# Earlier operand loads, own weight tiles on ScalarE's queue and evenly spread conversions in a fused attention and two-MLP kernel

## The chip, the cores and the metric

One core of a Trainium2 chip runs the whole kernel. The metric is device time in microseconds (us), the median of several executions; lower is better.

## What is computed

```
scores = q @ k^T / sqrt(64) - log(448)            # 4 batches, 12 heads, 448 x 64
x      = (sigmoid(scores) @ v), heads joined       # 1792 x 768
h      = x @ w_in1;  g = h * sigmoid(h)            # 768 -> 2048
x2     = g @ w_out1                                # 2048 -> 768
h      = x2 @ w_in2                                # 768 -> 2048
g      = P(h) / (Q(h) + 1e-6)                      # P cubic in h, Q quadratic in |h|
out    = g @ w_out2                                # 1792 x 768
```

The weights arrive as the bits of 64-bit floats. Every fp32 product is made of three fp32r matmuls: each operand is split into a high part (a cast on ScalarE, ACT) and a low part (a subtraction on VectorE, DVE, or on GpSimd, POOL), and high x high, high x low and low x high are added in PSUM.

## The kernel before

Each engine works through its instructions in the order in which the program lists them; the order is written by hand, and a transfer is issued by the queue of the engine that it is written for. SP's queue (SyncE) carries nearly every transfer of this kernel. The stages, in order:

**Conversions.** `conv` (lines 141 to 163) turns one 128 x 768 piece of a weight matrix from 64-bit bits into fp32: ACT takes an absolute value (line 150), DVE does four operations (lines 151, 152, 153, 156), SP stores the result to DRAM (line 159, tensors `w0i`, `w0o`, `w1i`, `w1o`), and `conv_load` has SP fetch the piece after next (lines 133, 137). The result sits in one of the three tiles of the ring `bits`. There are 64 pieces: 16 of `w_in1`, 16 of `w_out1` (`w0o`), 32 of the second MLP. The calls are spread by hand over the first three stages.

**Attention** (loop at line 766): 24 pairs of heads `i`, each in two half steps `h`. A half step transposes q or k of a later pair (line 235, through one PSUM bank that line 238 must have drained), does two score blocks (line 245, sigmoid at line 256) and two value blocks (line 263). From pair 13 on, each half step also takes one of the 21 steps of `operands0` (lines 330 to 354), which prepares operands of the next stage: three rounds `kk` of seven operands; a round starts with three loads of attention output from DRAM (`load_b`, line 324, SP's queue) into the tiles `wf[1][0]`, `wf[1][1]` and `s34f`, the same three tiles in each round, and the first step of the round casts the first of them at once (line 283 ACT, 284 DVE). From pair 1 to 20 the first half step of a pair ends with a `conv`.

**The seven-product stage** (loop at line 821): `x @ w_in1` by a recursion with seven half-size products instead of eight, in 16 groups `g`, nine matmuls to a product. The groups 0 to 7 make tokens of batches 0 and 1, the groups 8 to 15 those of batches 2 and 3. `silu` stores the results to DRAM (`gd`, line 431, SP). Conversions stand in groups 1, 3, 5 and 9 to 15. Its end prepares the next stage: `load_wo1` (line 524, SP's queue, into a tile of `bits`) and `split_wo1` (lines 287, 288) for the first pieces of `w_out1`, `load_g` (line 510, SP's queue) and `split_gd` (lines 283, 284) for the first pieces of g.

**The second product** (`second(n)`, lines 540 to 549): 64 steps `n`, 16 to a batch, each of 18 matmuls (lines 546 to 548) from one piece of g and one piece of `w_out1`. The pieces 0 and 1 of `second` stand inside the end of the stage before; the loop at line 926 has steps 2 to 63. In step `n` it loads g for step `n + 3` and `w_out1` for step `n + 2`, splits both for step `n + 1`, and calls `conv` at line 936 whenever twice the number of conversions left is at least the number of steps left: that is in each of the steps 2 to 14, then in every other step. `w_out1` is split only in the first 16 steps; later batches use it again.

**The second MLP** (from line 950) reads the stored result back and runs 64 steps of two products. Nothing in it is changed.

Of the kernel before, what the change touches and what calls it, by code (L numbers as in the profile page):

```python
# [41 lines left out]
def attention_moe_moe(ctx: ExitStack, tc: tile.TileContext, q, k, v, w_in1, w_out1, w_in2, w_out2, a, b2, out):  # L42
    nc = tc.nc
# [278 lines left out]
    def load_b(dst, t, half, kk, second):  # L322
        b = 2 * t + second
        nc.sync.dma_start(out=dst, in_=xs[0][half * HK + kk][:, b * S : (b + 1) * S])

    def split_b(src, t, kind, kk):
        x = xop[t, kind, kk] = place[t, kind, kk]
        split(src, x)

    def operands0():  # L330
        x, y, z = wf[1][0][:, :S], wf[1][1][:, :S], s34f[:, :S]
        for kk in range(HK):
            load_b(x, 0, 0, kk, 0)
            load_b(y, 0, 0, kk, 1)
            load_b(z, 0, 1, kk, 1)
            split_b(x, 0, "11", kk)
            yield
            sub(x, y, x)
            split_b(x, 0, "T1", kk)
            yield  # L340
            sub(y, z, y)
            split_b(y, 0, "T3", kk)
            load_b(y, 0, 1, kk, 0)
            yield
            split_b(z, 0, "22", kk)
            yield
            sub(x, z, x)
            split_b(x, 0, "T2", kk)
            yield
            split_b(y, 0, "21", kk)  # L350
            yield
            sub(y, y, x)
            split_b(y, 0, "T4", kk)
            yield
# [154 lines left out]
    def load_g(n):  # L509
        if n < B * KF:  # L510
            b, c = divmod(n, KF)
            gq[n] = f448.get()
            nc.sync.dma_start(out=gq[n], in_=gd[c][b])

    def split_gd(n):
        if n < B * KF:
            t = gq.pop(n)
            gx[n] = hl.get()
            split(t, gx[n])
            f448.put(t)  # L520

    wo_in = {}

    def load_wo1(c):
        if c < KF:
            wo_in[c] = bits.get()
            nc.sync.dma_start(out=wo_in[c], in_=wd[0][c]["o"])

    def split_wo1(c):
        if c < KF:  # L530
            t = wo_in.pop(c)
            split2(t, woH[c], woL[c])
            bits.put(t)

    ring8 = (0, 1, 3, 4, 5, 7, 2, 6)

# [193 lines left out]
    with tc.manual_schedule():  # L730
# [32 lines left out]
                attn_E(i)  # L763

        first_ops = operands0()
        for i in range(NPT):
            for h in range(2):
                if h == 0:
                    mix(i + 2)
                    load_v(i + 3)  # L770
                    load_qk(i + 4)
                attn_S(i, 2 * h, attn_QK(i, 2 * h))
                p = attn_QK(i, 2 * h + 1)
                if h == 0:
                    if i == 0:
                        attn_T(1, "k")
                    attn_T(i + 1, "q")
                else:
                    hl.put(st.pop(("k", i)), st.pop(("q", i)))
                    attn_T(i + 2, "k")  # L780
                attn_S(i, 2 * h + 1, p)
                behind(*((i, 0) if h else (i - 1, 1)))
                if i >= 2 * NP + 1:
                    next(first_ops, None)
                if i == NPT - 3 and h == 0:
                    load_w1(0)
                flush()
                if i == NPT - 2 and h == 1:
                    prep_ij(0)
                    sums_12(0)  # L790
                if i == NPT - 1:
                    if h == 0:
                        prep_s12(0)
                    else:
                        prep_a22(0)
                if h == 0 and 0 < i < NPT - 3:
                    conv()
        for _ in first_ops:
            pass
# [21 lines left out]
        for g in range(NGR):  # L821
# [28 lines left out]
                operands1_late("T1")  # L850
            if fill:
                next(ops1, None)
            if g in (1, 3, 5) or g > HF:
                conv()

            p6(g)
# [17 lines left out]
                operands1_late("T3")  # L874
            if fill:
                next(ops1, None)
            if last - 3 < g < last:
                split_wo1(g - last + 2)
            if g == last:
                split_gd(0)  # L880

            if was:
# [1 line left out]
            flush()  # L884
            load_w1(g + 2)
            sums_12(g + 1)
            if last - 4 < g < last:
                load_wo1(g - last + 3)
            if g == last:
                load_wo1(3)  # L890
                split_gd(1)

            p7(g)
# [17 lines left out]
        c12(last)  # L911
        w1_s.close()
        xb_s.close()
        kt_s.close()
        wo_p, wo_s = opened("wo")
        for c in range(2, KF):
            woH.append(wo_p.tile([P, DM], F32R, tag=f"woH{c}", name=f"woH{c}"))
            woL.append(wo_p.tile([P, DM], F32R, tag=f"woL{c}", name=f"woL{c}"))
        l2_p = ctx.enter_context(tc.tile_pool(name="l2a", bufs=1, side="right", reuse_waits="tile"))
        hx.put(*fixed("hx", KD, [P, 2, BK], F32R, l2_p))  # L920
        wi_f.extend(fixed("wif", 4, [P, DM], F32, l2_p))
        split_wo1(2)
        split_gd(2)
        load_g(4)
        NL1 = B * KF
        for n in range(2, NL1):
            load_g(n + 3)
            load_wo1(n + 2)
            second(n)
            split_gd(n + 1)  # L930
            split_wo1(n + 1)
            if n % KF == KF - 1:
                results1(n // KF)
            left = NL1 - 6 - n
            if left > 0 and (len(order) - done["conv"]) * 2 >= left:
                conv()
            m = n - (NL1 - KF)
            if m == 1:
                whr.put(w0[:2], w0[2:])
# [76 lines left out]
```

## Time and profile before

| | us |
|---|---|
| median of 3 runs (1182.17 to 1184.47) | 1183.79 |
| the profiled execution | 1185.87 |
| its span, first to last instruction | 1184.1 |
| TensorE (PE) busy in the span | 1119.8 (95%) |
| DVE, ACT, POOL busy | 864.3, 633.7, 340.4 |
| mean granted TensorE clock, of full speed | 0.971 |

A stage is read here from windows: the stretch of time, the busy time of each engine in it, the clock that TensorE was granted (1.00 is 2.4 GHz, 0.50 is 1.2 GHz), and the share of the time that the 16 DMA engines were busy. Where PE's busy time is shorter than the stretch, PE waited; the waits tell for whom.

### The profile page before, as it was taken

How to read it: one execution, taken by the hardware profiler on the slowest of the kernel's cores; microseconds unless marked ns; L12 is line 12 of the kernel's file. 1: busy time of each engine (PE TensorE's matmuls, PEld its weight loads, DVE VectorE, ACT ScalarE, POOL GpSimd, SP SyncE). 2: the span in 40 equal slices, each digit the busy share in tenths (PEclk: the TensorE clock that was granted, in tenths of full speed). 3: DMA queues.
4: the chain of work that ended last, by engine and by line, in shares of the span. 5: the costliest groups of instructions: out<-in, count | busy, mean ns of one | idle time of the engine just before them, and what ended most of it. 6: DMA issues, size and time to landing. Idle time of an engine off the chain costs nothing.

```text
span 1184.1 us, 15844 instructions
## 1 busy us (share of the span) xinstructions
PE 1119.8 (95%) x5822; PEld 926.9 (78%) x5822; DVE 864.3 (73%) x1028; ACT 633.7 (54%) x1035; POOL 340.4 (29%) x246
## 2 busy tenths in 40 slices
PE   9997888999999978779999999999999999999997
PEld 5553434898889967559999898888999988889997
DVE  4665675677777826666574638888899988788996
ACT  6775666555655623232232326546666665556664
POOL 2111110000000000000000015565677666566774
PEclk9998998999989988789999999999999999999999
DMA  9998774576547747778785829000100010001001
GB/s 249 306 291 240 233 233 153 160 253 205 183 149 240 241 143 244 261 250 278 265 289 202 310 81 385 23 21 21 44 11 28 27 40 1 21 21 54 1 1 40
DMA packets 103805, 183.47 MB, mean 155 GB/s; under 512 B 8752, under 2 KB 77872, under 8 KB 103728
## 3 DMA queue, kind: packets, MB, share of 16 engines
q1 hardware_dynamic: 103024, 181.86, 47.4%
q8 instruction: 46, 0.75, 0.3%
q10 hardware_dynamic: 640, 0.59, 0.2%
q14 instruction: 31, 0.25, 0.1%
q0 software_dynamic: 64, 0.00, 0.0%
HBM read 126.06 MB, written 56.36 MB: 154 GB/s over the span
## 4 chain that ended last, share of the span: by engine, by line
PE 78%; DVE 8%; DMA 7%; ACT 4%; issue 2%; SPq 1%; POOL 0%; ACTq 0%; DVEq 0%; POOLq 0%
PE acc L677 13%; PE acc L411 10%; PE acc L680 7%; PE hb L608 6%; PE hb L606 6%; PE hb L607 6%; PE hb L263 5%; PE pair L245 4%; PE acc L547 4%; PE acc L548 4%; PE acc L546 4%; PE hb L411 3%; PE hb L235 2%; DVE bits L153 2%; DMA f<-gd 1%
## 5 line engine op out<-in xcount | busy, mean ns | idle before, releaser
L288 POOL TENSOR_TENSOR w<-wif,w 128x768 fp32r<-128x768 f32 x33 | 61.3, 1858 | 516.8 <-DVE hx L591 509.4
L256 ACT ACTIVATE f<-pair,nls 112x896 f32<-112x896 f32 x96 | 96.5, 1010 | 19.0 <-PE pair L245 19.0
L546 PE MATMUL acc<-xa,woH 128*128 128x448 f32 x252 | 95.4, 379 | 0.5 <-ACT xa L283 0.5
L547 PE MATMUL acc<-xa,woH 128*128 128x448 f32 x252 | 95.2, 378 | 0.2 <-DVE xa L284 0.2
L548 PE MATMUL acc<-xa,woL 128*128 128x448 f32 x252 | 94.6, 375 | 0.0
L263 PE MATMUL hb<-f,vs 112*64 112x448 f32 x384 | 88.2, 582 | 0.4 <-ACT f L256 0.4
L245 PEld LDWEIGHTS pair<-xa,xa 64*112 64x112 f32 x576 | 48.3, 178 | 51.3 <-issue 34.4
L283 ACT CAST xa<-f 128x448 fp32r<-128x448 f32 x64 | 35.9, 564 | 96.7 <-DMA f<-gd 96.5
L634 DVE RECIPROCAL stg<-stg 128x512 f32<-128x512 f32 (+1 forms) x28 | 84.9, 3032 | 0.0
L245 PE MATMUL pair<-xa,xa 64*112 64x448 f32 x576 | 74.6, 390 | 9.6 <-ACT f L256 9.6
L621 ACT ACTIVATE stg<-hb,absb 128x512 f32<-128x512 f32 (+1 forms) x44 | 28.0, 636 | 98.2 <-PE hb L608 98.2
L284 DVE TENSOR_TENSOR xa<-f,xa 128x448 fp32r<-128x448 f32 x64 | 40.1, 641 | 46.5 <-ACT xa L283 46.2
L411 PE MATMUL acc<-xb,wr 128*128 128x448 f32 x315 | 67.8, 366 | 0.2 <-ACT f L485 0.2
L150 ACT ACTIVATE bits<-stg 128x768 f32<-128x768 f32 x64 | 57.9, 905 | 16.4 <-DMA w1i<-bits 8.4
L288 POOL TENSOR_TENSOR wh<-wif,wh 128x768 fp32r<-128x768 f32 x31 | 57.4, 1850 | 28.2 <-DVE xio L626 25.5
L411 PEld LDWEIGHTS acc<-xb,wr 128*128 128x128 f32 x315 | 59.1, 188 | 5.8 <-issue 0.7
L153 DVE SCALAR_TENSOR_TENSOR bits<-stg,bits 128x768 int32<-128x768 int32 x64 | 61.7, 964 | 2.2
L156 DVE SCALAR_TENSOR_TENSOR bits<-stg,bits 128x768 int32<-128x768 int32 x64 | 61.6, 962 | 2.2
L677 PE MATMUL acc<-w,hx 128*128 128x512 f32 x174 | 61.4, 394 | 0.0
L677 PE MATMUL acc<-wh,hx 128*128 128x512 f32 x171 | 60.3, 393 | 0.0
L288 POOL TENSOR_TENSOR w<-wof,w 128x768 fp32r<-128x768 f32 x32 | 59.2, 1850 | 0.4 <-ACT w L287 0.2
L288 POOL TENSOR_TENSOR wh<-wof,wh 128x768 fp32r<-128x768 f32 x32 | 59.2, 1850 | 0.1
(197 smaller groups left out, 3189.6 us busy)
## 6 DMA issues: line engine op xcount, KB each, us to landing
stg<-in_moe_w_in_dram SPq DMA_DIRECT2D x32, 768.0 KB, 6.2
stg<-in_moe_w_out_dram SPq DMA_DIRECT2D x32, 768.0 KB, 5.4
gd<-f SPq DMA_DIRECT2D x64, 224.0 KB, 3.4
f<-gd SPq DMA_DIRECT2D x64, 224.0 KB, 5.8
wf<-w0i SPq DMA_DIRECT2D x32, 384.0 KB, 5.9
w0i<-bits SPq DMA_DIRECT2D x16, 384.0 KB, 4.0
w0o<-bits SPq DMA_DIRECT2D x16, 384.0 KB, 2.7
bits<-w0o SPq DMA_DIRECT2D x16, 384.0 KB, 6.2
```

What stands on the lines that cost most here:

```text
L153: nc.vector.scalar_tensor_tensor(out=ui, in0=hi, scalar=SIGN_TOP, in1=ui, op0=ALU.bitwise_and, op1=ALU.bitwise_or)
L245: nc.tensor.matmul(p[:CP, j, :S], K[rows[j], a_, c * CP : (c + 1) * CP], Q[rows[j], b_, :], start=(n == 0), stop=(n == 2),)
L256: nc.scalar.activation(t[:CP], p[:CP, :, :S], AF.Sigmoid, bias=nls[:CP], scale=QKSCALE)
L263: nc.tensor.matmul(pav[0][j * D : (j + 1) * D, :S], vs[i][:, j, c * D : (c + 1) * D], t[:CP, j], start=(c == 0), stop=(c == NCH - 1),)
L288: (eng or nc.vector).tensor_tensor(out=lo, in0=src, in1=h.bitcast(F32), op=ALU.subtract)
L411: nc.tensor.matmul(o, w_[:, w], x[:, i_, :], start=first and kk == 0 and n_ == 0, stop=kk == HK - 1 and n_ == 2, skip_group_check=not first,)
L546: nc.tensor.matmul(o, woH[c][:, w], x[:, 0, :], start=(c == 0), stop=False)
L547: nc.tensor.matmul(o, woH[c][:, w], x[:, 1, :], start=False, stop=False)
L548: nc.tensor.matmul(o, woL[c][:, w], x[:, 0, :], start=False, stop=(c == KF - 1))
L634: nc.vector.reciprocal(t0, t1)
L677: nc.tensor.matmul(acc[t][:, :BK], a_, w_[:, :BK], start=first, stop=last)
L680: nc.tensor.matmul(rest, a_, w_[:, BK:], start=first and u == 0, stop=last and u == share - 1)
```

## The change

Four edits. First, `operands0` alternates between two sets of three tiles, and the loads that open a round move out of it into `load0`, called at half steps counted back from the end of the loop: rounds 0 and 1 at the two half steps of pair 11, round 2 at the first half step of pair 17. The 21 steps of `operands0` begin one half step earlier, at the second half step of pair 12. The fourth load of a round, in its third step, stays where it was. Second, `load_g` and `load_wo1` are issued by ACT's queue instead of SP's, and `w_out1` gets four tiles of its own, `wos`, where the tiles `kept` of the stage before were; in the second product it is loaded four steps before it is split (into the tile that was just split) and g is loaded for step `n + 2`, not `n + 3`. Third, the conversions: one more in attention (pair 21), groups 0, 2, 4, 6 instead of 1, 3, 5, and in the second product a steady rate, 32 of them over the steps 3 to 58. Fourth, the tiles `hx` and `wi_f` of the second MLP are opened at step 15, when `wos` is closed.

```diff
+    sets = ((wf[1][0], wf[1][1], s34f), (wf[0][0], wf[0][1], s12f))
+
+    def load0(kk):
+        x, y, z = (t[:, :S] for t in sets[kk % 2])
+        load_b(x, 0, 0, kk, 0)
+        load_b(y, 0, 0, kk, 1)
+        load_b(z, 0, 1, kk, 1)
+
     def operands0():
-        x, y, z = wf[1][0][:, :S], wf[1][1][:, :S], s34f[:, :S]
         for kk in range(HK):
-            load_b(x, 0, 0, kk, 0)
-            load_b(y, 0, 0, kk, 1)
-            load_b(z, 0, 1, kk, 1)
+            x, y, z = (t[:, :S] for t in sets[kk % 2])
             split_b(x, 0, "11", kk)
...
-            nc.sync.dma_start(out=gq[n], in_=gd[c][b])
+            nc.scalar.dma_start(out=gq[n], in_=gd[c][b])
...
-            wo_in[c] = bits.get()
-            nc.sync.dma_start(out=wo_in[c], in_=wd[0][c]["o"])
+            wo_in[c] = wos.get()
+            nc.scalar.dma_start(out=wo_in[c], in_=wd[0][c]["o"])
...
-                if i >= 2 * NP + 1:
+                at_half = 2 * i + h - 2 * NPT
+                if at_half >= -NOPS - 2:
                     next(first_ops, None)
-                if i == NPT - 3 and h == 0:
+                for kk, when in enumerate((-NOPS - 5, -NOPS - 4, -NOPS + 6 + 1)):
+                    if at_half == when:
+                        load0(kk)
+                if at_half == -6:
                     load_w1(0)
...
-                if h == 0 and 0 < i < NPT - 3:
+                if h == 0 and 0 < i < NPT - 2:
                     conv()
...
-            if g in (1, 3, 5) or g > HF:
+            if g in (0, 2, 4, 6) or g > HF:
                 conv()
...
-            if last - 3 < g < last:
-                split_wo1(g - last + 2)
             if g == last:
+                split_wo1(0)
+                load_wo1(4)
                 split_gd(0)
...
-            if last - 4 < g < last:
-                load_wo1(g - last + 3)
+            if g == last - 1:
+                kt_s.close()
+                wos_p, wos_s = opened("wos", side="right")
+                wos.put(*fixed("wos", 4, [P, DM], F32, wos_p))
+                for c in range(4):
+                    load_wo1(c)
             if g == last:
-                load_wo1(3)
+                split_wo1(1)
+                load_wo1(5)
                 split_gd(1)
...
         split_wo1(2)
+        load_wo1(6)
         split_gd(2)
-        load_g(4)
         NL1 = B * KF
+        todo = len(order) - done["conv"]
         for n in range(2, NL1):
-            load_g(n + 3)
-            load_wo1(n + 2)
+            load_g(n + 2)
             second(n)
             split_gd(n + 1)
-            split_wo1(n + 1)
+            if n + 1 < KF:
+                split_wo1(n + 1)
+                load_wo1(n + 5)
+            if n == KF - 1:
+                wos_s.close()
+                l2_p = ctx.enter_context(tc.tile_pool(name="l2a", bufs=1, side="right", reuse_waits="tile"))
...
-            left = NL1 - 6 - n
-            if left > 0 and (len(order) - done["conv"]) * 2 >= left:
-                conv()
+            conv_to(len(order) - todo + todo * (n - 1) // (NL1 - 7))
```

## Rows read from the trace of the kernel before

**Rows 1.** Windows, whole kernel: stretch, length, busy per engine, clock, DMA share, GB/s

```profile
75.00:100.00 25.00, 25.00 (x170) 12.98 (x168) 17.35 (x26) 20.12 (x26) 4.36 (x8) 1.00 1.03 296
104.00:211.30 107.30, 85.65 (x503) 41.06 (x501) 64.52 (x98) 65.64 (x92) 10.46 (x14) 0.89 0.62 198
211.30:421.30 210.00, 205.17 (x992) 187.91 (x990) 156.25 (x259) 117.30 (x217) 0.00 (x0) 0.98 0.62 206
421.30:442.40 21.10, 14.67 (x55) 12.15 (x54) 4.26 (x8) 5.47 (x11) 0.00 (x0) 0.84 0.32 122
442.40:532.00 89.60, 68.21 (x252) 55.33 (x253) 61.27 (x83) 29.96 (x43) 0.00 (x0) 0.83 0.78 253
550.00:575.00 25.00, 25.00 (x122) 22.60 (x121) 16.58 (x25) 7.78 (x12) 0.00 (x0) 1.00 0.76 265
```

**Rows 2.** Windows, attention from pair 13: each starts with a q transpose (line 235)

```profile
101.84:116.51 14.67, 8.12 (x50) 3.96 (x49) 5.59 (x9) 5.59 (x8) 1.84 (x3) 0.82 0.64 199
116.51:127.51 11.00, 9.61 (x49) 4.60 (x49) 7.49 (x12) 7.78 (x11) 1.63 (x2) 0.77 0.71 213
127.51:136.23 8.72, 7.23 (x49) 3.71 (x49) 6.51 (x11) 6.42 (x9) 1.81 (x2) 1.00 0.82 241
136.23:145.23 9.00, 7.25 (x48) 3.71 (x49) 6.66 (x10) 5.05 (x7) 1.64 (x2) 1.00 0.72 236
...
159.39:167.74 8.35, 7.25 (x48) 3.74 (x49) 6.65 (x11) 6.31 (x9) 1.25 (x2) 1.00 0.90 279
...
197.60:211.28 13.68, 13.25 (x82) 5.66 (x81) 7.58 (x12) 10.87 (x15) 0.00 (x0) 1.00 0.17 62
```

**Rows 3.** Waits, 100 to 210 us: engine, line, releaser: total us, times, longest

```profile
PE hb L235 <- DVE xa L238: 11.7, 8, 2.0
...
ACT xb L283 <- DMA wf<-xs: 18.0, 3, 7.4
ACT xb L283 <- DVE wf L302: 14.0, 9, 2.0
```

**Rows 4.** Timeline, PE, steps 0 and 2 of the second product, with the idle time before

```profile
424.40 0.47 PE L546 MATMUL hb<-xa,w 128*128 128x448 f32 x1 [3.06 <-ACT xa L283]
...
442.42 0.73 PE L546 MATMUL hb<-xa,woH 128*128 128x448 f32 x1 [2.51 <-ACT xa L283]
```

**Rows 5.** Waits, 442 to 533 us, second product steps 2 to 15

```profile
PE hb L546 <- ACT woH L287: 19.4, 8, 3.5
...
ACT woH L287 <- DMA bits<-w0o: 39.5, 12, 3.9
...
SPq L159 <- DVE bits L156: 62.3, 13, 5.0
```

**Rows 6.** Window of six us after one such wait: clock behind the POOL column

```profile
484.28:490.28 6.00, 6.00 (x16) 4.96 (x17) 4.51 (x6) 2.01 (x3) 0.00 (x0) 0.50 0.74 258
```

**Rows 7.** Groups by line, 442.4 to 532 us: count, busy us, mean ns, idle before

```profile
L288 DVE TENSOR_TENSOR woL<-bits,woH 128x768 fp32r<-128x768 f32 x14 | 13.4, 958 | 12.7 <-ACT woH L287 12.7
L156 DVE SCALAR_TENSOR_TENSOR bits<-stg,bits 128x768 int32<-128x768 int32 x13 | 12.5, 958 | 0.5
L284 DVE TENSOR_TENSOR xa<-f,xa 128x448 fp32r<-128x448 f32 x15 | 9.2, 618 | 0.0
L151 DVE TENSOR_SCALAR bits<-bits 128x768 f32<-128x768 f32 x13 | 7.3, 559 | 15.1 <-ACT bits L150 15.1
...
L150 ACT ACTIVATE bits<-stg 128x768 f32<-128x768 f32 x13 | 11.7, 901 | 16.4 <-DMA w1i<-bits 8.4 <-DMA w0o<-bits 4.3 <-DMA w1o<-bits 3.8
L287 ACT CAST woH<-bits 128x768 fp32r<-128x768 f32 x13 | 10.8, 832 | 39.5 <-DMA bits<-w0o 39.5
L283 ACT CAST xa<-f 128x448 fp32r<-128x448 f32 x14 | 7.8, 557 | 0.0
```

**Rows 8.** Line 513 (loads of g): landing time over the kernel; transfers issued by ACT

```profile
DMA to landing us min/median/max: 2.7/5.8/9.1
...
0.74 0.95 ACTq L180 DMA_DIRECT2D qs<-in_q_dram  x2
```

More of the change, by code (lines that the diff above doesn't have):

```diff
@@ L522, in attention_moe_moe @@
     wo_in = {}
+    wos = Ring([])
     def load_wo1(c):
         if c < KF:
-            wo_in[c] = bits.get()
-            nc.sync.dma_start(out=wo_in[c], in_=wd[0][c]["o"])
+            wo_in[c] = wos.get()
+            nc.scalar.dma_start(out=wo_in[c], in_=wd[0][c]["o"])
     def split_wo1(c):
@@ L532, in split_wo1 @@
             split2(t, woH[c], woL[c])
-            bits.put(t)
+            wos.put(t)
     ring8 = (0, 1, 3, 4, 5, 7, 2, 6)
@@ L765, in attention_moe_moe @@
         first_ops = operands0()
+        NOPS = 7 * HK
         for i in range(NPT):
@@ L913, in attention_moe_moe @@
         xb_s.close()
-        kt_s.close()
         wo_p, wo_s = opened("wo")
@@ L918, in attention_moe_moe @@
             woL.append(wo_p.tile([P, DM], F32R, tag=f"woL{c}", name=f"woL{c}"))
-        l2_p = ctx.enter_context(tc.tile_pool(name="l2a", bufs=1, side="right", reuse_waits="tile"))
-        hx.put(*fixed("hx", KD, [P, 2, BK], F32R, l2_p))
-        wi_f.extend(fixed("wif", 4, [P, DM], F32, l2_p))
         split_wo1(2)
+        load_wo1(6)
         split_gd(2)
-        load_g(4)
         NL1 = B * KF
+        todo = len(order) - done["conv"]
         for n in range(2, NL1):
-            load_g(n + 3)
-            load_wo1(n + 2)
+            load_g(n + 2)
             second(n)
             split_gd(n + 1)
-            split_wo1(n + 1)
+            if n + 1 < KF:
[4 more added lines that the diff above has]
+                l2_p = ctx.enter_context(tc.tile_pool(name="l2a", bufs=1, side="right", reuse_waits="tile"))
+                hx.put(*fixed("hx", KD, [P, 2, BK], F32R, l2_p))
+                wi_f.extend(fixed("wif", 4, [P, DM], F32, l2_p))
             if n % KF == KF - 1:
                 results1(n // KF)
-            left = NL1 - 6 - n
-            if left > 0 and (len(order) - done["conv"]) * 2 >= left:
-                conv()
+            conv_to(len(order) - todo + todo * (n - 1) // (NL1 - 7))
             m = n - (NL1 - KF)
```

## The prediction

> **What bounds the kernel now.** Read the windows first. Where nothing disturbs it, TensorE is busy for the whole of a stretch (first and last window of [rows 1]): there only less matmul work could help. The lost time lies in four places, as PE's busy time against the length of the stretch. Attention from 104 to 211 us has 85.65 us of work in 107.30. The seven-product stage loses only 4.8 us in 210. The hand-over from 421.3 to 442.4 has 14.67 in 21.10, and the second product's steps 2 to 15 have 68.21 in 89.60. The clock column adds to it: 0.89, 0.84 and 0.83 there, so part of the busy time is matmuls at 1.2 GHz. The rest of the second product and, by its unchanged code, the second MLP are taken as PE-bound.
>
> Then ask what ends last in each place. In attention ACT waited three times for an operand load, 18.0 us, up to 7.4 us each, because the round's cast stands right behind its loads; ACT's queue holds the sigmoids that PE needs next. Beside that, PE waited eight times, 11.7 us, for line 238, which on DVE stands behind a conversion [rows 3]. In the second product's first batch PE waited for the weight cast, the cast 39.5 us for its load, and SP, which issues that load, 62.3 us for DVE to end a conversion [rows 5]: one loop of conversion, store, weight load and split, turned once a step.
>
> **Attention.** The steps from pair 13 to 22 take 197.60 - 101.84 = 95.76 us. Pairs without a load wait and at full clock take 8.35 us (first step of the pair without a subtraction) or 8.72 and 9.00 (with one; mean 8.86) [rows 2]. The wait for line 238 is in these figures and stays. After the change the rounds' loads lie three, nine and five half steps ahead; at some 4.2 us each a half step is longer than a landing of 5.8 (half of it), so two half steps cover one. Pairs 13 to 21 each have two operand steps and a conversion: four of them at 8.35 and five at 8.86, 77.7 us, and 0.3 us for the step that moves into pair 12 (an ACT cast and a DVE subtraction of 0.56 and 0.62 us [rows 7], half beside other work). Gain 95.76 - 78.0 = 17.8 us. Pair 22 to the end keeps its 13.68 us: it gets two operand steps and loses one after it. Bounds: 12, if the pairs all take 9.0 and one load is still waited for (81 + 0.3 + 3); 22, if the waits on line 238 shrink by half as well. The six early loads (6 x 224 KB, at 296 GB/s 4.6 us of transfer) fall where the DMA engines are already full (first window of [rows 1]); they delay the loads of q, k and v, which are issued three or four pairs ahead, so I put that at nothing; without that cover it is 4.6 us, once.
>
> **Seven-product stage.** Conversions move between groups and one is added, 3.0 us of DVE each (two of 0.56 and two of 0.96 [rows 7]) where DVE is busy 156 of 210 us [rows 1]. Group 0 has two products less to hide behind and its conversion stands ahead of the low part that the last product of the group needs. Four transfers issued from ACT in group 14 cost ACT four times 0.47 us, by the two that it issued at the start in 0.95 [rows 8]. I take 1 us lost; bounds -1 and 4 (one conversion fully exposed, and 1 for ACT).
>
> **Hand-over and first batch**, 421.3 to 532.1 us, 110.8 us now. A step of 18 matmuls takes 25.0 / 122 x 18 = 3.69 us when PE is full (last window of [rows 1]), a product of nine 1.84. After the change:
> - Steps 0 and 1 and two products: 2 x 3.69 + 2 x 1.84 = 11.1 us. The wait of 3.06 us ahead of step 0 [rows 4] goes: ACT requests g behind its own copies in group 15, not behind SP's queue of stores and conversions; I leave 0.2.
> - The wait ahead of step 2, 2.51 us [rows 4], grows: between the cast of the weights and the cast of g, ACT now has a transfer into the tile that DVE must first finish (line 288, 0.96), and its issue (0.47). With hops 4.2 us. After such a wait the clock is 0.50 for about 6 us [rows 6], which costs 3.
> - Steps 2 to 15 at 3.69: 51.7 us, if weights and g keep up. Up to step 10 ACT must wait in each step for DVE's line 288 before it may issue the weight load, and behind that stand the next casts and the conversion's absolute value. A pair of steps with one conversion then goes round as: conversion 3.04, low part of g 0.62, of the weights 0.96, issue 0.47, next step's issue 0.47, casts 0.56 and 0.83, low part 0.96, issue 0.47, absolute value 0.90, together 9.3 us against 7.4 of PE. Four such pairs lose 8 us. What ACT is ahead at the start (about 3 us) and one more spell at half clock (3 us) cancel. After step 10 there is no such wait, and DVE's share, 0.62 + 0.96 + 0.56 x 3.04 = 3.3 us a step, fits.
>
> Together 11.1 + 0.2 + 4.2 + 3 + 51.7 + 8 = 78.2 us: a gain of 32.6. Bounds: 44 (no loss in the steps, 66.4 with the wait and without the clock) and 19 (each of nine steps is a full chain with its conversion, 3.04 + 0.62 + 0.96 + 0.47 + 0.90 = 6.1 us with hops, 22 us lost instead of 8).
>
> From step 16 on the wait of ACT is for g alone. The weight tiles and the 13 conversions that went first now come later, at 0.56 a step; PE hides them, as it now hides 0.5. I put it at nothing. Its cover is the landing time: two g loads are under way at a time and ACT's own work between them is 0.56 + 0.56 x 0.90 = 1.06 us, so a step takes (1.06 + landing) / 2, at the median 5.8 us [rows 8] 3.4, just under 3.69.
>
> The Trainium skill, "DMA: Bandwidth & Descriptors", section "Issuing engines are not separate DMA queues", says that transfers started from several engines run on the same 16 DMA engines, and that one saves only the time to initiate them. Taken alone that speaks against moving loads to ACT, as the landing would stay at 5.8 us. But the time that goes is the 62.3 us that SP stood waiting, which is neither initiation nor transfer; by the rule the sum would be some 3 us smaller, with the median landing instead of one nearer the least, 2.7.
>
> **The sum.** -17.8 + 1 - 32.6 = -49.4 us, on the profiled execution's 1185.87 us: 1136.5. That execution was 2.08 us above the median of 1183.79, so I forecast 1134 us.
>
> **Rivals.**
> 1. *The new waits on ACT bind* (the upper bound of the loop): the first batch gains 19 instead of 33, attention 14: 1152 us. For it speaks that ACT and DVE then wait for one another in each step and that DMA demand in steps 2 to 10 is 224 + 384 KB of loads plus half a conversion's 1152, 1.2 MB in 4.2 us, about the 296 GB/s that filled the DMA engines in attention. Against it: ACT is busy for a third of that stretch. Chance 0.17.
> 2. *No loss is left*: 66 us for hand-over and first batch, attention 20: about 1119 us. Against it stands that the wait ahead of step 2 must grow. Chance 0.13.
> 3. *Slower than before*: g's shorter lead. One step of lead instead of two makes all 48 steps from 16 on wait if the landing exceeds 2 x 3.69 - 1.06 = 6.3 us; at 9.1 us, the longest landing seen [rows 8], a step takes 5.1 us and 48 steps lose 68 us, and the first batch loses its gain of some 20 beyond the waits: about 1220 us. With both losses it is slower than before from a mean landing of about 7.9 us. For it: 5.8 is close to 6.3. Against it: those 5.8 us include transfers of 768 KB queued ahead on the same queue, and ACT can run up to seven tiles ahead of PE. Chance 0.04.
> 4. *The loads do not come early*: in attention the full DMA engines or a queue wait hold `load0` back and ACT waits as long as now: only the other part remains, 1152 us. For it: a DMA share of 1.03 just there. Against it: three half steps and more of room. Chance 0.06.
>
> The forecast has 0.60. The range takes in rivals 1, 2 and 4 as far as the bounds of the terms go: 1118 to 1153. About 0.2% is what a measurement of this kernel can tell from no change; faster by more than that 0.94, within it 0.02, slower 0.04.
>
> **What the changed profile would show.** Right: no ACT wait for line 324 between pairs 12 and 22, pairs of 8.3 to 9.0 us at clock 1.00; attention ending near 194 us. PE's step 0 without a wait, a wait of about 4 us ahead of step 2; steps 2 to 15 in 58 to 66 us, with ACT waiting for DVE's line 288; from step 16 on PE full. Wrong: ACT casts of g (line 283) waiting in step after step with PE behind them (rival 3), pairs that still take 11 us or more (rival 4), or a loss of more than 4 us more in the seven-product stage.

## The result, and the profile after

The changed kernel takes **1148.34 us** (median of four runs, 1145.94 to 1149.21), the kernel before 1183.56 beside it: a ratio of 0.970 with a 95% interval of 0.9683 to 0.9718. It is 35 us faster; the forecast was 1134, its range 1118 to 1153. The profiled execution took 1145.94 us, its span is 1144.2.

The line numbers have moved: loads of g are line 518, weight loads 533, the second product's matmuls 552 to 554, the seven-product matmuls 416. Windows of the kernel after, one for each stage of [rows 1] (columns as there): attention from pair 13, the seven products, the hand-over to step 2, steps 2 to 15, and two quiet-looking stretches of later steps.

```profile
100.00:195.00 95.00, 83.47 (x530) 41.14 (x526) 69.52 (x106) 69.41 (x97) 12.71 (x16) 0.96 0.80 247
195.03:409.90 214.87, 205.12 (x993) 187.88 (x991) 159.65 (x265) 118.92 (x219) 0.00 (x0) 0.98 0.64 212
409.90:428.98 19.08, 13.08 (x55) 11.18 (x53) 4.31 (x8) 5.02 (x10) 0.00 (x0) 0.91 0.34 130
428.98:489.30 60.32, 55.75 (x253) 48.34 (x254) 42.92 (x58) 24.52 (x38) 0.00 (x0) 0.97 0.75 246
525.00:550.00 25.00, 25.00 (x122) 22.70 (x122) 14.62 (x23) 7.06 (x13) 0.00 (x0) 1.00 0.81 270
625.00:650.00 25.00, 23.52 (x116) 21.30 (x115) 16.70 (x25) 10.16 (x17) 0.00 (x0) 1.00 0.86 290
```

Read PE's busy time against the length, as before. Steps 2 to 15 take 60.32 us instead of 89.60 and lose 4.6 instead of 21.4; the clock there rose from 0.83 to 0.97. The seven-product stage is the one that got worse: 214.87 us with 9.75 lost. The last window, steps 52 to 59, loses 1.5 us.

Attention: windows by pair of the kernel after, from pair 13, each from a q transpose to the next; then a wait from 90 to 200 us (engine, line, releaser: total us, times, longest).

```profile
102.22:111.61 9.39, 7.27 (x51) 3.73 (x49) 6.79 (x10) 5.61 (x8) 1.43 (x2) 1.00 1.10 290
111.61:120.39 8.78, 8.78 (x49) 4.18 (x49) 6.80 (x11) 6.53 (x10) 1.23 (x2) 0.81 1.04 301
120.39:128.30 7.91, 7.27 (x50) 3.75 (x49) 6.12 (x10) 6.29 (x9) 1.23 (x2) 1.00 0.95 274
...
136.66:145.97 9.31, 7.27 (x49) 3.62 (x49) 7.18 (x12) 7.79 (x11) 1.84 (x2) 1.00 0.95 279
145.97:156.39 10.42, 8.88 (x48) 4.11 (x49) 6.80 (x11) 6.42 (x9) 1.63 (x2) 0.84 0.71 244
...
182.17:195.03 12.86, 12.86 (x80) 5.84 (x81) 7.43 (x12) 11.08 (x15) 0.00 (x0) 1.00 0.37 129
```

```profile
PE hb L235 <- DVE xa L238: 11.5, 8, 2.1
```

The pairs of 14.67 and 11.00 us of [rows 2] are gone, and with them every ACT wait for an operand load, the 18.0 us of [rows 3]. The wait on line 238 stays (11.5 against 11.7). Two pairs ran partly at half clock (0.81 and 0.84).

The second product: timeline of the kernel after (start, duration, engine, line, operation, idle time before it). PE's step 2, SP's stores of three converted pieces, and one weight load with the cast of g behind it.

```profile
428.98 0.47 PE L552 MATMUL hb<-xa,woH 128*128 128x448 f32 x1 [4.00 <-ACT xa L283]
...
439.79 0.32 SPq L159 DMA_DIRECT2D w1i<-bits  x1
...
448.97 0.32 SPq L159 DMA_DIRECT2D w1o<-bits  x1
...
458.30 0.32 SPq L159 DMA_DIRECT2D w1i<-bits  x1
...
441.20 0.33 ACTq L533 DMA_DIRECT2D wos<-w0o  x1
...
442.18 0.57 ACT L283 CAST xa<-f 128x448 fp32r<-128x448 f32 x1 [4.39 <-DVE woL L288]
```

Waits of the kernel after from 428 to 490 us, the successor of [rows 5].

```profile
SPq L159 <- DVE bits L156: 53.8, 7, 13.1
...
ACT xa L283 <- DVE woL L288: 11.2, 4, 4.4
ACT xa L283 <- DMA f<-gd: 10.9, 5, 3.1
...
ACT bits L150 <- DVE woL L288: 6.0, 4, 1.8
...
PE hb L552 <- ACT xa L283: 4.0, 1, 4.0
...
PE hb L553 <- DVE xa L284: 2.3, 3, 1.2
```

PE's 19.4 us of waiting for the weight cast are gone, and so is ACT's wait for weight loads. In its place stands the new wait that the weight load brought: ACT stands for DVE's line 288 before it may issue into the tile, 11.2 us with the cast of g next behind it and 6.0 us with a conversion's absolute value (line 150) next, 17.2 us together. SP still waits for DVE, 53.8 us.

Where the time went, stage by stage, in every profiled execution. A stage begins with its first matmul: attention's end (from the start of the span), from there to step 0 of the second product, steps 0 and 1, steps 2 to 15, and the rest; the medians and ratios are those of the timed runs.

| kernel | attention | to step 0 | steps 0, 1 | steps 2-15 | rest | median us | ratio to before |
|---|---|---|---|---|---|---|---|
| before | 211.3 | 213.1 | 18.0 | 89.7 | 652.0 | 1183.6 | |
| after | 195.0 | 214.9 | 19.1 | 60.3 | 654.9 | 1148.3 | 0.970 (0.9683 to 0.9718) |
| early_loads | 194.6 | 210.3 | 17.8 | 89.5 | 650.4 | 1163.8 | 0.9835 (0.9819 to 0.9852) |
| spread_only | 210.1 | 210.2 | 17.2 | 79.9 | 660.0 | 1181.9 | 0.9991 (0.9979 to 1.0002) |
| dense_again | 193.5 | 215.6 | 17.3 | 69.9 | 649.5 | 1149.3 | 0.9721 (0.9702 to 0.9740) |
| sp_queue | 195.2 | 218.1 | 17.9 | 75.4 | 729.2 | 1236.7 | 1.0453 (1.0431 to 1.0475) |
| group3_for_2 | 194.5 | 209.6 | 18.9 | 61.5 | 653.9 | 1139.3 | 0.9621 (0.9598 to 0.9644) |
| load_at_start | 196.9 | 216.6 | 17.5 | 54.7 | 651.8 | 1139.1 | 0.9617 (0.9593 to 0.9641) |
| g_lead | 195.9 | 215.4 | 17.6 | 61.7 | 652.4 | 1144.9 | 0.9676 (0.9645 to 0.9707) |
| halves | 185.5 | 216.1 | 18.9 | 61.3 | 651.9 | 1135.8 | 0.9595 (0.9573 to 0.9617) |
| all_early | 185.6 | 212.3 | 15.7 | 53.6 | 665.5 | 1136.8 | 0.9616 (0.9584 to 0.9648) |
| all_even | 185.2 | 213.5 | 15.7 | 55.7 | 655.0 | 1120.3 | 0.9468 (0.9435 to 0.9502) |
| sp_lead3 | 196.0 | 220.0 | 18.3 | 54.5 | 652.8 | 1142.5 | 0.9659 (0.9631 to 0.9687) |
| sp_lead3_dense | 194.7 | 222.0 | 19.0 | 66.6 | 651.7 | 1153.9 | 0.9739 (0.9718 to 0.9761) |

How far a stage can be trusted: the stage to step 0 has the same code in before, early_loads and spread_only and took 213.1, 210.3 and 210.2 us. Differences under 3 us between two single profiles are therefore not read as effects.

### The profile page after: what moved, and what is told of

It is laid out like the page before. It is cut to its first block, busy times and chain, and to the rows that moved or that the text cites. A ratio compares the mean times of both kernels' runs of the same rounds, so it can differ in the third digit from the quotient of the medians.

```text
span 1144.2 us, 15865 instructions
## 1 busy us (share of the span) xinstructions
PE 1100.3 (96%) x5822; PEld 917.0 (80%) x5822; DVE 865.0 (76%) x1028; ACT 633.0 (55%) x1035; POOL 341.8 (30%) x246
## 4 chain that ended last, share of the span: by engine, by line
PE 77%; DMA 9%; DVE 7%; ACT 3%; issue 2%; SPq 1%; ACTq 1%; POOL 0%; DVEq 0%; POOLq 0%
PE acc L683 14%; PE acc L416 9%; PE acc L686 7%; PE hb L614 7%; PE hb L613 7%; PE hb L612 7%; PE hb L263 5%; PE pair L245 4%; PE acc L553 3%; PE acc L554 3%; PE acc L552 3%; PE hb L416 3%; DMA f<-gd 2%; PE hb L235 2%; PE hb L554 1%
## 5 line engine op out<-in xcount | busy, mean ns | idle before, releaser
L288 POOL TENSOR_TENSOR w<-wif,w 128x768 fp32r<-128x768 f32 x33 | 61.7, 1869 | 489.5 <-ACT w L287 484.6
L256 ACT ACTIVATE f<-pair,nls 112x896 f32<-112x896 f32 x96 | 96.7, 1012 | 18.3 <-PE pair L245 18.2
L553 PE MATMUL acc<-xa,woH 128*128 128x448 f32 x252 | 93.2, 370 | 3.1 <-DVE xa L284 3.1
L552 PE MATMUL acc<-xa,woH 128*128 128x448 f32 x252 | 93.0, 369 | 0.0
L263 PE MATMUL hb<-f,vs 112*64 112x448 f32 x384 | 85.2, 567 | 0.0
L156 DVE SCALAR_TENSOR_TENSOR bits<-stg,bits 128x768 int32<-128x768 int32 x64 | 63.1, 986 | 2.2
L153 DVE SCALAR_TENSOR_TENSOR bits<-stg,bits 128x768 int32<-128x768 int32 x64 | 62.9, 983 | 2.2
L151 DVE TENSOR_SCALAR bits<-bits 128x768 f32<-128x768 f32 x64 | 36.1, 564 | 32.8 <-ACT bits L150 32.4
L683 PE MATMUL acc<-wh,hx 128*128 128x512 f32 x171 | 60.3, 393 | 0.0
```

The source lines that it names most:

```text
L256: nc.scalar.activation(t[:CP], p[:CP, :, :S], AF.Sigmoid, bias=nls[:CP], scale=QKSCALE)
L263: nc.tensor.matmul(pav[0][j * D : (j + 1) * D, :S], vs[i][:, j, c * D : (c + 1) * D], t[:CP, j], start=(c == 0), stop=(c == NCH - 1),)
L288: (eng or nc.vector).tensor_tensor(out=lo, in0=src, in1=h.bitcast(F32), op=ALU.subtract)
L552: nc.tensor.matmul(o, woH[c][:, w], x[:, 0, :], start=(c == 0), stop=False)
L553: nc.tensor.matmul(o, woH[c][:, w], x[:, 1, :], start=False, stop=False)
L683: nc.tensor.matmul(acc[t][:, :BK], a_, w_[:, :BK], start=first, stop=last)
```

## The experiments

### What each part brings

**The loads of attention alone**, on the kernel before (`sets`, `load0` and `at_half`; nothing else).

```diff
+                for kk, when in enumerate((-NOPS - 5, -NOPS - 4, -NOPS + 6 + 1)):
+                    if at_half == when:
+                        load0(kk)
```

> Only the first edit, on the kernel before: rounds of operand loads begun early into two sets of tiles, operand steps one half step earlier. Theory (the three load waits on ACT cost attention its time): attention ends near 195 us as in the changed kernel, 16 us earlier than before, and the later stages keep their lengths (210 us for the seven products, 111 us from its end to step 16 of the second product): about 1167 us. Rival (the early loads only move the wait to the full DMA engines, and attention gained by something else): 1180 us or more.

1163.8 us: attention ends at 194.6 instead of 211.3. The stage to step 0 is 2.8 us shorter with the same code, which is within the scatter; the others lie where they were before. So this edit is worth 19.5 us by the medians, 16.7 by the stage, and it owes nothing to the other three.

**The even spread of the conversions alone**, on the kernel before.

```diff
-            left = NL1 - 6 - n
-            if left > 0 and (len(order) - done["conv"]) * 2 >= left:
-                conv()
+            conv_to(len(order) - todo + todo * (n - 1) // (NL1 - 7))
```

> Only the even spread of the conversions over the second product, on the kernel before: weight and g loads stay on SP's queue and in the shared tiles. Theory A (the loop of conversion, store, load and split is turned once for each conversion, and both tiles and queue matter): steps 2 to 15 hold 8 conversions instead of 13; steps with one keep about 6.4 us, those without take 3.7: 16 us saved, about 1168 us. Theory B (the spread alone is what the changed kernel gains here): 31 us saved, about 1152 us.

1181.9 us, no change that can be told. Steps 2 to 15 gain 9.8 us, and the rest gives 8.0 back; neither theory foresaw that. Waits of this kernel in its steps 2 to 15 (437.4 to 517.3 us), and two windows late in the second product:

```profile
ACT woH L287 <- DMA bits<-w0o: 42.9, 9, 9.4
```

```profile
641.00:666.00 25.00, 22.02 (x102) 18.50 (x101) 15.41 (x24) 6.70 (x11) 0.00 (x0) 1.00 0.87 312
666.00:691.00 25.00, 22.41 (x106) 19.31 (x105) 20.20 (x25) 8.82 (x15) 4.66 (x2) 1.00 0.71 249
```

ACT waits for the weights as long as before, 42.9 us against the 39.5 of [rows 5], though 8 conversions are in the way instead of 13, and one wait is now 9.4 us long. So it isn't only the number of conversions that made the weights late. The windows show PE losing 5.6 us late in the second product, where conversions that went early before now stand beside the loads of the second MLP (the DMA engines move 312 GB/s in the first); that these loads are the reason is not shown.

**The change with the conversions as they were.**

```diff
+            left = NL1 - 6 - n
+            if left > 0 and (len(order) - done["conv"]) * 2 >= left:
+                conv()
-            conv_to(len(order) - todo + todo * (n - 1) // (NL1 - 7))
```

> The changed kernel with the conversions of the second product put back to one in each of the first steps. Theory A (own tiles and ACT's queue alone do not do it: a conversion in every step makes a round of 6.1 us while weight loads last, to step 10, and 4.7 us of DVE after): steps 2 to 15 take some 78 us instead of 60, about 1166 us. Theory B (the tiles and the queue were what mattered): within 3 us of the changed kernel, 1148 us.

1149.3 us, the time of the change. The spread is again worth 9.6 us in steps 2 to 15, and again it costs in the rest, 5.4 us; by the medians nothing is left of it. (The rule gives this kernel 11 conversions in those steps, to the 13 of the kernel before, because it has 32 left and not 34.)

**The change with g and the weights issued by SP.**

```diff
-            nc.scalar.dma_start(out=gq[n], in_=gd[c][b])
+            nc.sync.dma_start(out=gq[n], in_=gd[c][b])
-            nc.scalar.dma_start(out=wo_in[c], in_=wd[0][c]["o"])
+            nc.sync.dma_start(out=wo_in[c], in_=wd[0][c]["o"])
```

> The changed kernel with g and the weights loaded by SP's queue again, own tiles and even spread kept. Theory A (SP's queue is blocked behind the conversion's store until DVE ends it, with g now only one step ahead): steps 2 to 15 lose 10 us against the changed kernel, about 1158 us. Theory B (tiles and spread suffice): 1148 us. Theory C (ACT is better off without the issues and the waits that they carry): 1143 us.

1236.7 us, 88 more than the change and 4.5% more than before; theory A had the direction, but 1158. Waits of this kernel from 510 to 680 us, and a window in the middle of that:

```profile
ACT xa L283 <- DMA f<-gd: 132.8, 20, 9.7
...
SPq L159 <- DVE bits L156: 126.0, 18, 10.4
```

```profile
556.00:581.00 25.00, 19.74 (x85) 16.72 (x84) 11.97 (x17) 5.05 (x8) 0.00 (x0) 0.93 0.55 190
```

This is rival 3 of the prediction, on the other queue: the rest takes 729.2 us, 74 more than after (the rival's price was 68). With a load of g only two steps ahead and a conversion's store ahead of it in the same queue, the store waits up to 10.4 us for DVE and g comes up to 9.7 us late. What this run doesn't tell is which of the two, the queue or the lead, is to blame; the last pair of runs does.

### What the change left lying

**The conversion of group 2 put into group 3.** In the kernel after, group 2 of the seven products looks as follows on the timeline (DVE ends the conversion; SP; ACT; PE):

```profile
225.37 0.96 DVE L156 SCALAR_TENSOR_TENSOR bits<-stg,bits 128x768 int32<-128x768 int32 x1
226.36 0.32 SPq L159 DMA_DIRECT2D w0o<-bits  x1
226.77 0.38 SPq L137 DMA_DIRECT2D stg<-in_moe_w_out_dram  x1
...
228.22 0.45 SPq L324 DMA_DIRECT2D T<-xs  x1
...
234.92 0.56 ACT L283 CAST xa<-T 128x448 fp32r<-128x448 f32 x1 [8.94 <-DMA T<-xs]
...
239.51 3.73 PE L416 MATMUL acc<-xb,wq 128*128 128x448 f32 x9 [5.39 <-ACT f L490]
```

The store waits in SP's queue for DVE, a 768 KB fetch follows it, and behind both stands the load of an operand (`T`) that ACT must cast next. ACT waits 8.94 us, PE 5.39, and the six us after that ran at half clock, as a window of the same kernel shows:

```profile
239.50:245.50 6.00, 5.99 (x16) 5.34 (x17) 5.04 (x11) 4.16 (x8) 0.00 (x0) 0.50 0.47 162
```

```diff
-            if g in (0, 2, 4, 6) or g > HF:
+            if g in (0, 3, 4, 6) or g > HF:
```

> The changed kernel with one conversion moved: groups 0, 3, 4, 6 of the seven-product stage instead of 0, 2, 4, 6. Theory A (in group 2 the conversion's store waits on DVE in SP's queue, with the loads of the second round of operands1 and behind a 768 KB load, and ACT stands 8.9 us on them): the stage takes 210.3 us instead of 214.9, about 1144 us. Theory B (the loss is the sum of small delays of four conversions instead of three, and of the issues on ACT): the stage stays within 1 us of 214.9, 1148 us.

1139.3 us, 9 less than the change by the medians (5.8 by the profiled executions). The stage takes 209.6 us instead of 214.9. Waits of this kernel from 195 to 405 us:

```profile
ACT xa L283 <- DMA T<-xs: 8.4, 3, 4.0
```

In the kernel after the same line reads 15.2 us, with 8.9 the longest. The five kernels with the conversion in group 2 and ACT's queue average 215.7 us in this stage, the three with it in group 3 211.8.

**The weight load behind the load of g.** In the change ACT issues the weight load at the end of a step, ahead of the conversion's absolute value and the next load of g. Here it goes behind both, to the start of the next step, into the same tile and with the same lead.

```diff
         split_wo1(2)
-        load_wo1(6)
...
             load_g(n + 2)
+            load_wo1(n + 4)
             second(n)
             split_gd(n + 1)
             if n + 1 < KF:
                 split_wo1(n + 1)
-                load_wo1(n + 5)
```

> The changed kernel with each weight load issued at the start of the next step, four pieces ahead, when its tile has long been read, instead of right behind the split that empties the tile. Theory A (the waits of ACT for DVE's low part, once a step to step 10, make the pairs of 9.2 us): the wait ahead of step 2 falls from 4.0 to 2.6 us, steps 2 to 15 from 60.3 to 55 us, about 1141 us. Theory B (the pairs are set by the landing of g, one step ahead, or by full DMA engines): only the 1.4 us ahead of step 2, 1147 us.

1139.1 us. Steps 2 to 15 take 54.7 us instead of 60.3. Waits of this kernel from 431 to 490 us:

```profile
ACT xa L283 <- DVE woL L288: 14.2, 9, 3.2
PE hb L552 <- ACT xa L283: 2.5, 1, 2.5
...
PE hb L553 <- DVE xa L284: 0.3, 1, 0.3
```

ACT still waits 14.2 us for line 288 (17.2 in the change), none of it ahead of the absolute value any more. But PE's wait for the low part of g falls from 2.3 to 0.3 us, and the one ahead of step 2 from 4.0 to 2.5; these are 3.5 of the 5.6 + 1.5 us gained from there to step 16. Most of what remains is two smaller waits of PE that are gone (1.5 us for line 288, 0.5 for the weight cast) and PE's busy time (54.3 us in these steps instead of 55.7). The cost lay mainly in what stood behind the wait: the load of g and the absolute value.

**g one step earlier, still on ACT.**

```diff
+        load_g(4)
...
-            load_g(n + 2)
+            load_g(n + 3)
```

> The changed kernel with g loaded for step n + 3 again, as in the kernel before, still on ACT's queue. Theory A (on ACT's queue a landing of 4.1 us is covered by one step of lead): steps 2 to 15 gain at most 2 us, from step 16 to the end at most 3 us: 1144 to 1148 us. Theory B (the short lead costs in every step): the rest of the second product shortens by 6 us or more, 1142 us or less.

1144.9 us; the intervals of the two ratios overlap, so no gain is shown. The rest takes 652.4 us, within the scatter of the 651.8 and 651.9 that two kernels with the short lead have. On ACT's queue two steps are enough.

**The conversions of pairs 12 to 21 cut in two**, the absolute value and two DVE operations in the first half step, the other two with the store in the second.

```diff
-                if h == 0 and 0 < i < NPT - 2:
-                    conv()
+                if 0 < i < NPT - 2:
+                    if i < 2 * NP:
+                        if h == 0:
+                            conv()
+                    elif h == 0:
+                        conv_a()
+                    else:
+                        conv_b()
```

> The changed kernel with each conversion of pairs 12 to 21 in attention cut in two: the absolute value and the two first DVE operations at the first half step's end, the other two with the store at the second's. Theory A (PE's 11.5 us of waits for line 238 come from 3.0 us of conversion standing ahead of it on DVE): these waits nearly go, pairs fall from 8.4 to about 7.5 us, attention ends 8 us earlier, about 1140 us. Theory B (the pairs are limited by what ACT and DVE have to do at all, 7.1 and 6.9 us a pair, and by ACT's waits for the subtractions): attention gains under 3 us, 1146 us or more.

1135.8 us, 12.5 less than the change, and attention ends at 185.5 us instead of 195.0. Waits of this kernel from 100 to 186 us (its line 263 is the transpose of line 235, its line 266 the drain of line 238):

```profile
PE hb L263 <- DVE xa L266: 2.6, 7, 0.5
```

and its window over most of that stretch:

```profile
102.00:185.00 83.00, 78.42 (x512) 38.63 (x510) 67.30 (x104) 67.52 (x95) 11.47 (x16) 1.00 0.91 271
```

The wait on the drain falls from 11.5 us to 2.6, none is longer than 0.5, and the clock is 1.00 throughout. The 3 us of DVE that a conversion holds in one piece were what PE's transpose waited for.

### Together

**All four, and the conversions of the first batch thinned further**: half a conversion a step up to step 15, three quarters afterwards.

```diff
-            conv_to(len(order) - todo + todo * (n - 1) // (NL1 - 7))
+            conv_to(len(order) - todo + ((n - 1) // 2 if n < KF else 7 + (n - KF + 1) * 3 // 4))
```

> The changed kernel with four edits at once: group 3 instead of 2, weight loads at the start of the step, conversions of attention in halves, g loaded for step n + 3; and the conversions of the second product at one in two steps for the first batch, then three in four, so that they end at step 50 instead of 58. If the gains of the single runs add (9 + 9 + 12.5 + 3.5 us): about 1114 us; if the runs overlap where they shorten the same step (g's lead and the early weight loads): 1122 us. Steps 2 to 15 at 54 us, the time from step 16 to the end at 649 to 650 us, as in the run with dense conversions, if late conversions are what collides with the second MLP's first loads.

1136.8 us. The three stages ahead of step 16 take 281.6 us after attention, 12.7 less than in the change, but the rest takes 665.5. Waits and a window of this kernel from 467 us on (its line 581 is the second product's, its line 312 the subtraction of line 284):

```profile
PE acc L581 <- DVE xa L312: 10.8, 8, 2.8
...
ACT bits L150 <- DMA stg<-in_moe_w_in_dram: 27.1, 5, 8.0
```

```profile
467.20:642.90 175.70, 164.82 (x783) 148.25 (x782) 114.70 (x164) 53.80 (x88) 3.77 (x2) 0.98 0.79 264
```

At three quarters of a conversion a step PE loses 10.9 us of 175.7, nearly all in eight waits for the low part of g. That rate isn't hidden, and this is where the run's expectation failed. ACT's absolute value waits up to 8.0 us for its piece there, with the cast of g behind it; whether that is the link that holds PE, no run tells.

**The same four, with the even spread of the change.**

> The same as all_early but with the changed kernel's even spread of the conversions to step 58. Theory A (conversions after step 48 share SP's queue and ACT with the first loads of the second MLP): from step 16 to the end 652 to 654 us, 2 to 4 us more than all_early. Theory B (the time after step 16 does not depend on when the conversions end): the same time as all_early within 1 us.

**1120.3 us**, the fastest kernel here: ratio 0.9468 to before (0.9435 to 0.9502), 28 us under the change. Against both theories the time from step 16 on is 10.5 us shorter than in all_early. A stretch of 175.7 us from step 16 has 172.58 us of PE work:

```profile
470.10:645.80 175.70, 172.58 (x835) 156.28 (x834) 111.89 (x160) 52.22 (x87) 4.25 (x2) 1.00 0.76 257
```

The four edits alone gave 9, 9, 3.5 and 12.5 us by their medians, 34 if they added; together they give 28. The load of g stands ahead of ACT's wait now (steps 2 to 15 take 55.7 us), attention ends at 185.2, and the rest, at the even spread, is that of the change.

### Queue or lead

**The change with g and the weights on SP, and g three steps ahead as before** (the edits of the run on SP's queue and of the one on g's lead together).

> The changed kernel with g and weights on SP's queue, as in sp_queue, but g loaded for step n + 3 as before the change. Theory A (the short lead made sp_queue slow: each g load waits behind a conversion's store, and one step cannot cover both): steps from 16 on come back to about 655 us, some 1160 us in all. Theory B (SP's queue itself is too slow for the even spread): the time from step 16 on stays above 690 us, over 1195 us in all.

1142.5 us: not slower than the change, and beside the run with the same lead on ACT (1144.9) the same, as the intervals of their ratios overlap. Waits of this kernel from 430 to 650 us, then in its steps 2 to 15 alone, and the window of these steps:

```profile
SPq L159 <- DVE bits L156: 106.5, 30, 6.9
```

```profile
SPq L159 <- DVE bits L156: 22.2, 7, 5.5
```

```profile
434.26:488.80 54.54, 54.22 (x253) 49.65 (x254) 42.52 (x59) 24.25 (x38) 0.00 (x0) 0.94 0.83 283
```

SP waits for DVE up to 6.9 us at a time, with g and the weights behind that, and PE loses 0.3 us in steps 2 to 15. What SP's queue costs is at the hand-over: 220.0 us up to step 0 against 215.4 for the same lead on ACT. So one step more of lead for g is worth 94 us on SP's queue (1236.7 to 1142.5).

**The same with the conversions as they were**, to get own tiles without spread and without ACT's queue.

> As sp_lead3 (own weight tiles loaded four pieces ahead, but on SP's queue, g for step n + 3), with the conversions of the second product dense again, one in each of the first steps: what is left of the change in this stage is the own tiles and their longer lead. Theory A (the shared tiles made the loop; with own tiles a conversion in each step costs only DVE's time, 3.04 + 0.62 + 0.96 = 4.6 us a step): steps 2 to 15 take about 67 us, near the 70 of dense_again. Theory B (SP's queue, blocked in every step until DVE ends the conversion, makes the loop, tiles or not): about 85 us or more, as before the change (89.7).

1153.9 us, steps 2 to 15 in 66.6. With this run the stage can be laid out in full (us for steps 2 to 15; PE's own need is 51.7):

| | dense conversions | even spread |
|---|---|---|
| weights through `bits`, two steps ahead, SP, g three ahead | 89.7 | 79.9 |
| own tiles, four ahead, SP, g three ahead | 66.6 | 54.5 |
| own tiles, four ahead, ACT, g two ahead (the change) | 69.9 | 60.3 |

The tiles of their own with the longer lead bring 23 to 25 us, the spread 10 to 12, and ACT's queue with the shorter lead costs 3 to 6. g_lead (61.7 with g three ahead on ACT) and load_at_start (54.7) put that cost on the place of the weight load in ACT's order and not on the lead of g. The rows are not quite alike: the first has 13 conversions in these steps when dense and 8 when even, the others 11 and 7. At the 2 to 3 us that the spread gains for each conversion fewer (9.8 us for five, 12.1 and 9.6 for four), an estimate of 4 to 6 of the 23 us and 2 to 3 of the 25 is not the tiles'. Tiles and lead were not tried apart.

## Where the prediction was right and where not

The direction, the places and most of the mechanism held; the time came out 14.3 us above the forecast, inside the range. In the profiled pair the sum was -49.4 us forecast and -39.9 measured (spans 1184.1 and 1144.2):

| term | forecast | measured |
|---|---|---|
| attention | -17.8 | -16.3 |
| seven products | +1 | +4.8 |
| hand-over and first batch | -32.6 | -31.4 |
| from step 16 | 0 | +2.9 |

The seven products are taken from 211.3 to 421.3 us before, as in [rows 1]; the 213.1 of the table of stages holds the wait ahead of step 0 as well. Together these terms miss by 9.4 of the 14.3 us. The other 4.9 come from reading single executions: the profiled execution of before was slower than its median, so the forecast took off 2.5 us on the way to 1134, while the one of after was 2.4 us under its own.

**Attention: right.** Pairs 13 to 21 took 79.95 us (102.22 to 182.17) for 78.0, and ACT's wait for the loads went altogether; the excess is about that of the two pairs at reduced clock (2.0 us above the forecast's 8.35 and 8.86). Three pairs (9.39, 9.31 and 10.42 us) lie above the 9.0 that the prediction gave as the upper end. The loss of 11.5 us on line 238 was kept in the sum and stayed. The run with the cut conversions shows that it was to be had.

**Seven products: the term mis-sized, and for a wrong reason.** The prediction costed the moved conversions by DVE's 3.0 us and looked at group 0, where PE then waited only 0.25 us. It didn't follow the conversion's store: SP's in-order queue makes every load behind it wait for DVE (4.0 us here), and in group 2 those are loads of operands needed at once; the first of them then landed 6.7 us after its issue. The bound of 4 came from one exposed conversion; the loss was a late load and a spell at half clock. group3_for_2 took the stage from 214.9 to 209.6 us.

**Hand-over: right in the waits that it named.** No wait ahead of step 0; the wait ahead of step 2 was put at 4.2 us and is 4.00. A wait of 2.00 us inside step 0, after its first three matmuls, for DVE's `f` (line 305), was not foreseen, and matmuls at half clock follow it (0.91 in the window). So the stretch to step 2 took 19.08 us for the 15.5 forecast; the first batch fell short of its forecast by 2.4, so that the sum of the two came nearer than its parts, by luck. (The bound without loss is 11.1 + 0.2 + 4.2 + 51.7 = 67.2 us by the prediction's own terms, not 66.4; the gain of 44 stands.)

**First batch: the number nearly right, part of its reason wrong.** 62.7 us were forecast from step 2 to 16 (3 + 51.7 + 8), 60.3 measured. The chain of a pair of steps, 9.3 us in the prediction, is there: SP's stores come 9.18 and 9.33 us apart in the timeline above. That ACT's new wait costs PE time is shown by load_at_start, which moves work out from behind it and gains 5.6 us. But the prediction credited the gain to taking the loads off the queue in which SP waits 62.3 us for DVE. The runs contradict that. In the change SP still waits 53.8 us in these steps; with the weights back on SP's queue, the same tiles and the same lead of the weights, and g three steps ahead, loads stand behind waits of up to 5.5 us again and PE loses 0.3 us. What counted was how far ahead of its use a load is issued, which took tiles of its own.

Here the prediction argued against a rule of the Trainium skill ("DMA: Bandwidth & Descriptors", section "Issuing engines are not separate DMA queues"), that issuing from another engine saves only the time to initiate. The runs agree with the rule where the lead is long enough: 1142.5 us on SP and 1144.9 on ACT, both with g three steps ahead. They set it a limit that it doesn't speak of: with g two steps ahead the queue decides, 1236.7 against 1148.3, since a waiting store holds up what is behind it.

**From step 16: put at nothing.** PE loses 3.1 us in two waits for the subtraction of line 284, in steps 55 and 60; before lost 0.7 late in the second product. With the conversions dense again they are 0.6. The forecast's cover, that PE hides 0.56 conversions a step, held but for the last steps, where the second MLP's first work stands beside them (the wait in step 60 is looked at below). The rival of g's short lead did not happen: the landing of g was 4.6 us in the median and 7.8 at most, instead of 5.8 and 9.1 [rows 8], as line 518 of the kernel after shows:

```profile
DMA to landing us min/median/max: 2.5/4.6/7.8
```

**Of the rivals**, none describes the run as a whole: the loads did come early, ACT's new wait did bind, but at the size that the forecast had given it.

What stays open: why the rest of spread_only is 8.0 us longer than before, of which the two windows explain 5.6; why one and the same stage differs by 3 us between executions; and what the fourth edit does, since no run has it alone (its code stands at the end of step 15).

## What to carry to other kernels

Follow every DMA of a step that you move, not only its compute: in an in-order queue a store that waits for an engine delays each load behind it, so the lead of those loads has to cover the longest such wait. Give a load its own tile and enough lead before you give it another queue; on a compute engine's queue put it behind the work that others need soonest, since all that follows it waits with it. Long blocks on a shared engine are best cut at the point where another engine waits, even where the sum of the work stays the same.

## What the runs showed of the hardware

A DVE operation slowed by work on POOL was not in the prediction. In the kernel after, the last conversion's two operations with two operands from SBUF take 2.50 and 2.48 us while POOL splits its first weights; everywhere else in the second product they take 0.96, as before [rows 7]. The timeline from 650 us: DVE, then PE,

```profile
650.70 2.50 DVE L153 SCALAR_TENSOR_TENSOR bits<-stg,bits 128x768 int32<-128x768 int32 x1
653.23 2.48 DVE L156 SCALAR_TENSOR_TENSOR bits<-stg,bits 128x768 int32<-128x768 int32 x1
...
656.31 0.47 PE L553 MATMUL acc<-xa,woH 128*128 128x448 f32 x1 [1.58 <-DVE xa L284]
```

and POOL in the same time:

```profile
650.34 2.03 POOL L288 TENSOR_TENSOR w<-wif,w 128x768 fp32r<-128x768 f32 x1 [483.93 <-ACT w L287]
652.60 2.30 POOL L288 TENSOR_TENSOR w<-wif,w 128x768 fp32r<-128x768 f32 x1 [0.23 <-ACT w L287]
```

Each DVE operation starts just after one of POOL's and ends with a delay of 1.5 us; the next subtraction for PE is late by it, and PE waits 1.58 us. The Trainium skill ("SBUF — State Buffer", section "Who interferes with whom") says that a DVE instruction with two SBUF inputs contends with a GpSimd instruction that reads SBUF, and that the order of issue decides who is blocked. The trace agrees in that DVE's operation, which came second, is the long one: POOL's had 1.67 us left when DVE's began (650.34 + 2.03 - 650.70), and 1.67 + 0.96 = 2.63 us is near the 2.50.

Other runs take the two apart. In sp_lead3 the first of the last conversion's two operations starts ahead of POOL's and the second inside it:

```profile
649.49 0.96 DVE L153 SCALAR_TENSOR_TENSOR bits<-stg,bits 128x768 int32<-128x768 int32 x1
...
650.30 1.84 POOL L288 TENSOR_TENSOR w<-wif,w 128x768 fp32r<-128x768 f32 x1 [1.86 <-ACT w L287]
...
650.48 2.48 DVE L156 SCALAR_TENSOR_TENSOR bits<-stg,bits 128x768 int32<-128x768 int32 x1
```

In every kernel here the operations of a conversion that start inside one of POOL's first splits take 2.48 to 2.50 us (eleven, in seven kernels), and those of the second product that do not take 0.96; in before, early_loads, dense_again, sp_lead3_dense and all_early the last conversion ends before POOL's first split, and none is long. Only how the 2.5 us come about, the rest of POOL's operation and then DVE's own, is argued.
